# A gate of one element on GpSimd's queue, ahead of three of six early loads

## The chip, the cores and the metric

The kernel runs on one core of a Trainium2 chip. The metric is the device time of one execution in microseconds, the median over several runs. An execution's own time is a little longer than the span of its profile, which runs from the first to the last recorded instruction.

## The reference

The input is a sequence of 2048 rows with 512 features. Four residual layers follow one another: a convolution (A), a local attention (B), and both once more with the same weights. Each layer reads the layer norm of its input.

```python
def _A_ref(u, A_re, A_im, B_re, B_im, C_re, C_im, log_dt, Dskip):
    ...
    P = jnp.exp(logdA[:, :, None] * l[None, None, :])
    K = jnp.einsum("dn,dnl,dn->dl", Cc, P, dB).real      # one kernel of 2048 taps per feature
    ...
    Yf = Uf * Kf[None, :, :, :]                          # causal convolution by FFT of length 4096
    ...
def _B_ref(x, wqkv, wo):
    ...                                                  # 32 heads of 16; each row sees W=8 rows,
    logits = jnp.einsum("bhsd,bhswd->bhsw", q, kg) * scale   # 2 apart, itself and back
    attn = _softmax(logits, axis=-1)
    o = jnp.einsum("bhsw,bhswd->bhsd", attn, vg)
    return (lambda x, *d: x.transpose(*d))(o, 0, 2, 1, 3).reshape(B, S, D) @ wo

x = A_u
x = x + _A_ref(_layernorm(x, axis=-1), ...)
x = x + _B_ref(_layernorm(x, axis=-1), B_wqkv, B_wo)
x = x + _A_ref(_layernorm(x, axis=-1), ...)
x = x + _B_ref(_layernorm(x, axis=-1), B_wqkv, B_wo)
```

## The kernel before

The state `X` stays in SBUF as bf16, shaped 128 partitions × 16 slots × 512 features: row 16·p + j of the sequence is partition p of slot j. "The row sum of slot j" is the residual sum that the attention layer writes back into slot j of `X`.

The program has four stages, one per layer. `kernel_and_first_conv` builds the convolution kernels, transforms them and writes their spectra to DRAM, into `kt_scratch`: sixteen tiles, numbered (dc, c), with dc the feature block (0 to 3) and c a quarter of it. `b_layer` is the first attention, `a_layer` the second convolution, and `b_layer` again the second attention. `a_layer` doesn't build the spectra anew; it loads the sixteen tiles from `kt_scratch` into the tile `Kt`, for which there are eight buffers, and multiplies each with the transformed input (line 1172: `pa<-xc,Kt` on VectorE).

Each stage is written as a plan. `pl.op` notes an operation with its engine ("P" TensorE, "V" VectorE, "A" ScalarE, "G" GpSimd, "S" the DMA queue of SyncE, SP), an estimate of its time and what it depends on; `pl.either` notes several ways of doing one thing. `ORDERS` then holds, for each of the four plans, a list of operation numbers, written out ahead of time: it picks the way and fixes the order on every engine. The numbers count the operations as they are noted, ways not taken included. Semaphore waits follow from the data. As each engine works its queue in order across stages, instructions of the next stage can stand among those of the stage before, if the list of their stage and their place in the program's queue let them: GpSimd, with little to do, issues loads of `a_layer` while `b_layer` still runs.

A load of one tile (dc, c) is `load`, line 1222: two DMAs of 64 partitions each, 256 KB apiece, that put the tile's two planes into the upper and into the lower half of the partitions. For dc below 2 it is issued on GpSimd; the others go on SP, either in the same way (line 1222 as well) or as two smaller DMAs (line 1229) with two VectorE copies (line 1234) that fill in the other halves. Six loads are issued early on GpSimd, in the order (0,0), (0,3), (1,2), (1,1), (1,0), (1,3): twelve DMAs one behind another, once `kt_scratch` and the buffers are there. Two more early loads go on SP, after the last transposes of the attention. These eight fill the buffers; the other two loads of GpSimd, (0,1) and (0,2), wait until VectorE's products have freed theirs. The products run in the order (1,0), (1,3), (1,2), (1,1), (0,0), (0,3), and then the rest.

The end of `b_layer` is where the early loads run. VectorE multiplies values with weights (`prod`, line 1696), with four buffers for `prod`; TensorE sums the products in PSUM (`po`, lines 1711, 1720 and 1725). ScalarE writes `po` as bf16 into `ot` (line 1738), and a DMA on SP that transposes puts `ot` into `oT` (line 1743):

```python
nc.sync.dma_start(oT[:, fp, j * 256:(j + np) * 256].rearrange("f (b p) -> f b p", p=128),
                  box.pop(("ot", fp, j))[:, 0:np * 256], transpose=True)
```

Some parts of `oT` are written by TensorE and ScalarE instead (lines 1740 and 1753). TensorE multiplies `oT` with the output weights (`ps_o`, line 1808), and slot by slot the sum goes back to `X`. In the first attention, slots 8 to 15 are summed on VectorE in one of two ways, line 1783 straight from PSUM or line 1790 from a copy `sp` that ScalarE made (line 1787), or on TensorE, from where ScalarE copies it (line 1920). Slot 13 is the first of the two sums of line 1783. After it VectorE and ScalarE work out the norm of the rows (lines 200 to 229, 1930), which writes `U`, the input of `a_layer`. There, line 1118 begins the transform, the tile `Z` is transposed into `zt` on SP (line 1133) or by TensorE (line 1139), and the products follow.

`pst` holds statistics of the rows (lines 1360 and 1364), which the attention layers work out at their start; its part for slot 15 is not in use in the stretch that matters here.

Of the kernel before, what the change touches and what calls it, by code (L numbers as in the profile page):

```python
# [15 lines left out]
BF = mybir.dt.bfloat16  # L16
# [3 lines left out]
S = 2048  # L20
# [5 lines left out]
NJ = 16  # L26
# [95 lines left out]
def _bf(a):  # L122
    return np.ascontiguousarray(np.asarray(a, dtype=np.float32).astype(NPBF))
# [53 lines left out]
def b_weights(nc, const, wo):  # L177
    bones = const.tile([128, 4, 32], BF, name="sb_bones")
    wo_t = const.tile([128, 4, 512], BF, name="wo_t")
    VX = const.tile([128, 2, NV + NJ, 256], BF, name="VX")  # L180
    return dict(bones=bones, wo=wo_t, osrc=[wo[ft * 128:(ft + 1) * 128, :].rearrange("(h d) o -> d h o", d=DH) for ft in range(4)]), VX
# [50 lines left out]
def load_params(nc, pp, prm):  # L232
# [12 lines left out]

ORDERS = [
# [66 lines left out]
class Plan:  # L315
# [25 lines left out]
    def run(self):  # L341

        order = [int(i) for i in ORDERS[Plan.turn].split()]
        Plan.turn += 1
# [750 lines left out]
def a_layer(nc, tc, C, X, kt_dram, U):  # L1095

    with ExitStack() as es:
        vpool = es.enter_context(tc.tile_pool(name="a_vt", bufs=2))
        kp = es.enter_context(tc.tile_pool(name="a_kt", bufs=8, reuse_waits="tile"))
# [2 lines left out]
        zk = es.enter_context(tc.tile_pool(name="a_zt", bufs=6))  # L1102
        wk = es.enter_context(tc.tile_pool(name="a_wk", bufs=3))
        psA = es.enter_context(tc.tile_pool(name="a_psA", bufs=4, space=PSUM))
        ident, C2, IC, F1, F1T = C["ident"], C["C2"], C["IC2"], C["F1"], C["F1T"]
        Kl = {}
        pl = Plan(psA=4, Z=3, zt=6, xc=4, kt=8, pa=3, VT=2)
        box, zdone, tdone, vdone, Xq = {}, {}, {}, {}, {}
# [107 lines left out]
        def load(dc, c):  # L1216

            def go(eng):
                k = box["kt", dc, c] = kp.tile([128, 2, 1024], BF, name="Kt", tag="Kt")
                rows = kt_dram[dc, c]  # L1220
                for h in range(2):
                    eng.dma_start(k[64 * h:64 * h + 64], bass.AP(rows.tensor, rows.offset, [[1024, 64], [64 * 1024, 2], [1, 1024]]))
            if dc < 2:
                Kl[dc, c] = pl.op("G", 1.5, lambda: go(nc.gpsimd), pl.outer(("qk",)), take=("kt", dc, c), lag=4.0)
            else:
                def once():
                    k = box["kt", dc, c] = kp.tile([128, 2, 1024], BF, name="Kt", tag="Kt")
                    for h in range(2):
                        nc.sync.dma_start(k[64 * h:64 * h + 64, h], kt_dram[dc, c, 64 * h:64 * h + 64])

                def other():
                    k = box["kt", dc, c]
                    for h in range(2):
                        nc.vector.tensor_copy(k[64 - 64 * h:128 - 64 * h, h], k[64 * h:64 * h + 64, h])
                Kl[dc, c] = pl.either(("load", dc, c), lambda: pl.op("S", 1.15, lambda: go(nc.sync), take=("kt", dc, c), lag=4.0),
                                      lambda: pl.op("V", 0.84, other, pl.op("S", 1.15, once, take=("kt", dc, c), lag=3.5)))

        for dc in range(4):
            prev = []
            for j0, nj in ((0, 4), (4, 4), (8, 4), (12, 2), (14, 2)) if dc < 2 else ((0, 4), (4, 4), (8, 4), (12, 4)):  # L1240
                prev = [s1(dc, j0, nj, [pl.outer(("u", j)) for j in range(j0, j0 + nj)], *prev)]
            for c in range(4):
                load(dc, c)
            for c in range(4):
                turn(dc, c)
            for c in range(4):
                inverse(dc, c, product(dc, c, s2(dc, c)))
            nj = 4 if dc == 3 else 8
            for k in range(NJ // nj):
                final(dc, k, nj)  # L1250
# [3 lines left out]
def b_layer(nc, tc, C, X, Wt, VX, XT, pst, eps, ln, center, evac, done, VSTAT_Q):  # L1254

    with ExitStack() as es:
        oTp = es.enter_context(tc.tile_pool(name="b_oT", bufs=1))
        qk = es.enter_context(tc.tile_pool(name="b_qk", bufs=1))
# [16 lines left out]
        box = {}  # L1275
        pl = Plan(psA=2, psL=1, psO=2, prod=4, LT=3, sp=NSP, sm1=1, sm2=1, sm_m=1, sm_s=1, rdb=1)
# [498 lines left out]
        def tokens(fp, j, t, r):  # L1775
            if (fp, j // 8) == (1, 1):
                o = j * 256 + t * 128 + r
            else:
                o = j // 8 * 2048 + r * 16 + j % 2 * 256 + t * 128 + j % 8 // 2 * 32
            return oT[:, fp, o:o + 32]  # L1780
# [14 lines left out]
        def out(qt):  # L1795
            es = []
            for j in range(qt * 4, qt * 4 + 4):
                pool, ring = (psL, "psL") if j == 14 else (psO, "psO") if j == 15 else (psA, "psA")
                key = (ring, "o", j)

                def mm(begin, fts, res, j=j, pool=pool, ring=ring):
                    if begin:
                        box["o", j] = pool.tile([128, 512], F32, name="ps_o", tag=ring)
                    ps = box["o", j][:]
                    for ft in ([-1] if begin and res else []) + list(fts):
                        for r in range(0, 128, 32):
                            lhsT, rhs = (ident[:, r:r + 32], X[:, :, j, :]) if ft < 0 else (tokens(ft // 2, j, ft % 2, r), wo_t[:, ft, :])
                            nc.tensor.matmul(ps[r:r + 32], lhsT, rhs, start=(ft == -1 or ft == 0 and not res), stop=(ft == 3), skip_group_check=True)  # L1808

                def way(res, slow=False, j=j, key=key, mm=mm):  # L1810
                    if qt == 3:
                        a = pl.op("P", 0.68 if res else 0.46, lambda: mm(True, range(2), res), Od[0, j], Od["last", 1, 8], Wl.get("wo", []), take=key)
                        a = pl.op("P", 0.46, lambda: mm(False, range(2, 4), res), a, Od[1, j])
                    else:
                        a = pl.op("P", 1.14 if res else 0.91, lambda: mm(True, range(4), res), Od[0, j], Od[1, j], Wl.get("wo", []), take=key)
                    if res is None:
                        a = pl.op("A", 0.48, lambda: taken(j, box.pop(("o", j))[:]), a, take=("sp", j), drop=key)
                        if slow:
                            return pl.op("G", 1.2, lambda: summed_taken(j), a, lag=3.5, drop=("sp", j))
                        return pl.op("V", 0.33, lambda: added_taken(j), a, drop=("sp", j))  # L1820
                    fn = evac if res else added
                    return pl.op("A" if res else "V", 0.48 if res else 0.61,
                                 lambda: fn(j, box.pop(("o", j))[:]), a, drop=key)
                ways = [lambda: way(True), lambda: way(False)]
                es.append(pl.either(("out", j), *ways[::-1] if qt in ADD_Q else ways, lambda: way(None), lambda: way(None, True)) if qt in VSTAT_Q else way(True))
            done(pl, qt, es)

        if center:
# [45 lines left out]
def kernel(  # L1874
# [16 lines left out]
    nc = tc.nc  # L1891
    const = ctx.enter_context(tc.tile_pool(name="const", bufs=1))
    kt_dram = nc.dram_tensor("kt_scratch", (4, 4, 128, 1024), BF).ap()
    prm = dict(A_re=A_A_re, A_im=A_A_im, B_re=A_B_re, B_im=A_B_im, C_re=A_C_re, C_im=A_C_im, log_dt=A_log_dt,
               Dskip=A_Dskip)
    C = {}
# [5 lines left out]
    pst = const.tile([128, NJ, 2, 6], F32, name="pst")  # L1902
    X = kernel_and_first_conv(nc, tc, C, prm, A_u[0], const, kt_dram, eps, Wt)
    const2 = ctx.enter_context(tc.tile_pool(name="const2", bufs=1))
    ln = LnStats(nc, const2, [(0, D)], "a2", eps, "a2")
    ln.squares(const2)
    more, VX = b_weights(nc, const2, B_wo)
    for name, arr, dt in (("IC2", _bf(C["IC2"]), BF), ("minus", _bf(-np.eye(128)), BF), ("down", np.eye(128, k=1, dtype=np.float32), F32)):
        C[name] = load_const(nc, const2, name, arr, dt, nc.gpsimd)
    Wt.update(more)  # L1910
# [80 lines left out]
```

## Time and profile before

| | |
|---|---|
| median of 3 runs | 426.59 us (426.13 to 427.98) |
| profiled execution, own time | 428.47 us |
| profiled execution, span | 426.7 us |
| mean granted TensorE clock | 0.964 |
| busy: TensorE (PE), VectorE (DVE), ScalarE (ACT), GpSimd (POOL) | 83%, 92%, 77%, 7% |
| DMA queue of GpSimd's transfers (q0) | 3376 packets, 5.37 MB, 6.6% of 16 engines |
| DMA queue of SP's transfers (q1) | 97638 packets, 44.46 MB, 50.3% of 16 engines |

Times in a profile are counted from the span's start. A line such as L1696 is a line of the kernel before. A row of a timeline gives the start, the length, engine, line, operation, output and inputs, the count of instructions merged in it, and in brackets how long the engine sat idle before and who released it. SPq and POOLq are the queues from which SP and GpSimd issue DMAs. "To landing" is the time from the issue of a DMA until its completion is signalled.

### The profile page before, as it was taken

To read this page: it belongs to the slowest core of one execution; us is meant where nothing else is said; L and a number is where in the kernel's file an instruction comes from. 1 tells how busy PE (TensorE), PEld (TensorE's weight loads), DVE (VectorE), ACT (ScalarE), POOL (GpSimd) and SP (SyncE) were. 2 spreads that over 40 slices of the span, in tenths; PEclk is the share of its full clock that TensorE was granted. 3 is DMA by queue.
4 is the path that set the end of the run, shared out by engine and by line. 5 is a ranking of instruction groups with operands and counts; after the bars stand their busy time and mean duration, and the time that the engine had idled before them with its cause. 6 is when DMAs were issued, how large, how long until landed. Compare 5 with 4: busy or idle time off the path is not lost. (4 is left out here: it accounts for less than half of the span.)

```text
span 426.7 us, 13641 instructions
## 1 busy us (share of the span) xinstructions
PE 355.1 (83%) x5837; PEld 229.1 (54%) x5866; DVE 393.4 (92%) x652; ACT 326.5 (77%) x534; POOL 28.9 (7%) x98
## 2 busy tenths in 40 slices
PE   2259867987997889999985987899999999966994
PEld 1154655776786764446642533478774455642452
DVE  6999999999999788989999985999999999999994
ACT  7999999999998575579862794999976778762630
POOL 1000000000000200010000510020000010000321
PEclk9999989999999999999997996999999999995998
DMA  7996257697988775003335496099974000243496
GB/s 215 209 292 251 95 70 151 145 173 166 172 137 142 147 169 103 18 2 91 101 78 74 106 206 160 2 143 207 197 124 69 18 2 2 85 119 66 55 168 144
DMA packets 103538, 52.01 MB, mean 122 GB/s; under 512 B 82923, under 2 KB 95356, under 8 KB 103222
## 3 DMA queue, kind: packets, MB, share of 16 engines
q1 hardware_dynamic: 97638, 44.46, 50.3%
q0 software_dynamic: 3376, 5.37, 6.6%
q10 hardware_dynamic: 2464, 1.31, 1.1%
q8 instruction: 46, 0.75, 0.8%
q14 instruction: 14, 0.11, 0.1%
HBM read 19.30 MB, written 6.29 MB: 60 GB/s over the span
## 5 line engine op out<-in xcount | busy, mean ns | idle before, releaser
L1696 DVE TENSOR_TENSOR prod<-VX,L 128x512 bf16<-128x512 bf16 (+2 forms) x72 | 75.9, 1101 | 5.3 <-PE po L1725 4.8
L1520 DVE TENSOR_TENSOR prod<-qT,kT 128x4096 bf16<-128x4096 bf16 (+1 forms) x40 | 72.3, 1855 | 0.5 <-ACT kT L1426 0.3
L1808 PE MATMUL ps_o<-wo_t,oT 128*32 128x512 bf16 x512 | 34.2, 399 | 4.3 <-DMA oT<-ot 4.1
L1475 PE MATMUL ps_v<-wv,U 128*128 128x256 bf16 x256 | 31.6, 272 | 1.7 <-ACT VX L1486 1.0
L876 ACT CAST Z<-ps_s 128x1024 bf16<-128x1024 f32 (+1 forms) x36 | 32.0, 932 | 1.3 <-PE ps_s L873 1.1
L1421 PE MATMUL ps_qk<-U,wqk 128*128 128x512 bf16 x128 | 30.3, 380 | 0.7 <-ACT qT L1426 0.7
L1486 ACT ACTIVATE VX<-ps_v,rs 128x256 bf16<-128x256 f32 x64 | 26.8, 472 | 3.8 <-PE ps_v L1475 3.0
L1475 PEld LDWEIGHTS <-U 128*128 128x128 bf16 x256 | 24.5, 97 | 9.6 <-issue 5.1
L1440 PE MATMUL ps_qk<-U,wqk 128*128 128x512 bf16 x128 | 28.8, 379 | 0.8 <-ACT X L1210 0.8
L1531 PE MATMUL Lp<-prod,sb_bones 128*32 128x512 bf16 x256 | 22.8, 422 | 5.5 <-DVE prod L1520 5.5
L1738 ACT CAST ot<-po 128x1024 bf16<-128x1024 f32 (+1 forms) x15 | 14.4, 985 | 14.1 <-PE po L1711 10.5
L1808 PEld LDWEIGHTS <-oT 128*32 128x32 bf16 x512 | 13.3, 100 | 18.7 <-DMA oT<-ot 4.6
L1711 PE MATMUL po<-prod,sb_ident 32*32 32x512 bf16 x768 | 16.7, 419 | 8.0 <-DVE prod L1696 7.7
L1421 PEld LDWEIGHTS <-wqk 128*128 128x128 bf16 x128 | 11.8, 98 | 17.0 <-issue 4.8
L968 DVE TENSOR_TENSOR pa<-sp_u,sp_k 128x2048 bf16<-128x2048 bf16 x16 | 19.4, 1220 | 1.6 <-ACT sp_k L904 0.7
L1440 PEld LDWEIGHTS <-wqk 128*128 128x128 bf16 x128 | 12.4, 98 | 15.1 <-issue 1.1
L873 PE MATMUL ps_s<-KT,FK 128*128 128x128 bf16 (+1 forms) x360 | 18.8, 209 | 1.4 <-ACT KT L846 0.7
L1172 DVE TENSOR_TENSOR pa<-xc,Kt 128x2048 bf16<-128x2048 bf16 x16 | 18.9, 1219 | 0.6 <-PE vp L1184 0.3
L873 PEld LDWEIGHTS <-FK 128*128 128x128 bf16 x360 | 17.4, 98 | 3.0 <-issue 2.1
L893 PE MATMUL xp<-zt,sb_C 128*128 128x512 bf16 x45 | 15.2, 386 | 4.4 <-ACT zt L913 2.1
L982 PE MATMUL vp<-sb_IC,pa 128*128 128x128 bf16 x256 | 17.0, 219 | 2.2 <-DVE pa L968 1.2
L904 ACT CAST sp_k<-xp 128x1024 bf16<-128x1024 f32 x16 | 16.5, 1046 | 1.6 <-PE xp L893 0.7
(233 smaller groups left out, 864.4 us busy)
## 6 DMA issues: line engine op xcount, KB each, us to landing
kt_scratch<-sp_k SPq DMA_DIRECT2D x16, 256.0 KB, 3.1
Kt<-kt_scratch POOLq DMA_DIRECT2D x16, 256.0 KB, 7.1
sp_u<-sp_u SPq DMA_DIRECT2D x18, 128.0 KB, 2.8
X<-in_A_u_dram SPq DMA_DIRECT2D x8, 256.0 KB, 5.6
X<-in_A_u_dram SPq DMA_DIRECT2D x4, 512.0 KB, 5.2
Kt<-kt_scratch SPq DMA_DIRECT2D x8, 256.0 KB, 5.2
VX<-VX SPq DMA_DIRECT2D x4, 448.0 KB, 3.7
VX<-VX SPq DMA_DIRECT2D x4, 336.0 KB, 3.3
```

Of the source, the lines that this page charges most:

```text
L873: nc.tensor.matmul(ps[:, r, 0:n // 4, jj * 4:(jj + 1) * 4], w, x, start=(k == 0), stop=(k == len(todo) - 1))
L876: nc.scalar.copy(box["Z", kind, dc, b0][:, 0:n // 4, :, jq * 16:(jq + 1) * 16].rearrange("p g r k -> p r g k"), box.pop(("s1", kind, dc, j ...
L968: nc.vector.tensor_tensor(pr[:], box["U"][:, s:t + 1:t - s], k[:].unsqueeze(1).to_broadcast([128, 2, 1024]), ALU.mult)
L1172: nc.vector.tensor_tensor(pr[:], x[:].unsqueeze(1).to_broadcast([128, 2, 1024]), box.pop(("kt", dc, c))[:], ALU.mult)
L1421: nc.tensor.matmul(ps[:], wqk[:, ct, f0:f0 + 128], XT[:, ct // 2, 4 * s:4 * s + 4, ct % 2, :], start=(ct == 0), stop=(ct == 3))
L1440: nc.tensor.matmul(box[name][:, k * 512:k * 512 + 512], wqk[:, ct, f0:f0 + 128], XT[:, ct // 2, 4 * s:4 * s + 4, ct % 2, :], start=(ct == ...
L1475: nc.tensor.matmul(ps[:, jj].rearrange("p t h d -> p (t h d)"), XT[:, ct // 2, j + jj, ct % 2, :], wv[:, ct, fp * 256:(fp + 1) * 256], sta ...
L1486: nc.scalar.activation(out, ps, ACT.Identity, scale=r)
L1520: nc.vector.tensor_tensor(pr[:], windows(q, 0, 2), windows(kT[fp][:, a:a + n2, col(w):col(w) + 1024], -DIL * 128, 2), ALU.mult)
L1531: nc.tensor.matmul(Lp[r0:r0 + 32, w // 4, :], bones[:, w % 4 + k, :], pr[:, k, f2 - a, hb * 512:(hb + 1) * 512], start=(n == 1 and k == 0) ...
L1696: nc.vector.tensor_tensor(p2[:].rearrange("p w j t d h -> p w (j t) d h"), windows(v, -DIL * 256, taps), l.to_broadcast([128, taps, nj * 2 ...
L1808: nc.tensor.matmul(ps[r:r + 32], lhsT, rhs, start=(ft == -1 or ft == 0 and not res), stop=(ft == 3), skip_group_check=True)
```

## The change

A copy of one element on GpSimd reads partition 0, slot 13 of `X` and writes it into the unused part of `pst`. In the written-out order of the third plan it stands behind the third of the six early loads. It therefore waits for the sum in slot 13, and the last three early loads, (1,1), (1,0) and (1,3), stand behind it. As the copy reads slot 13, the later write of that slot (ScalarE, line 1210) waits for it in turn. The ways of a load are noted in another form, which shifts the numbers in the third list; the order on the other four engines stays as it was.

```diff
+GATES = (13,)
 ORDERS = [
...
-    "362 113 32 38 4 145 114 120 121 127 143 129 132 137 133 6 246 138 141 11 12 147 18 20 23 24 153 158 151 152 332 28 "
...
+    "388 127 32 47 4 165 52 128 134 135 141 160 143 146 151 147 6 272 152 155 11 12 170 18 20 23 24 179 184 177 178 358 "
...
+        held = C["held"]
...
+            key = ("kt", dc, c)
+            ways = [lambda: pl.op("S", 1.15, lambda: go(nc.sync), take=key, lag=4.0),
+                    lambda: pl.op("V", 0.84, other, pl.op("S", 1.15, once, take=key, lag=3.5))]
             if dc < 2:
-                Kl[dc, c] = pl.op("G", 1.5, lambda: go(nc.gpsimd), pl.outer(("qk",)), take=("kt", dc, c), lag=4.0)
...
+                ways.insert(0, lambda: pl.op("G", 1.5, lambda: go(nc.gpsimd), pl.outer(("qk",)), take=key, lag=4.0))
+            Kl[dc, c] = pl.either(("load", dc, c), *ways)
+
+        def gate(k, j):
+            pl.op("G", 0.1, lambda: nc.gpsimd.tensor_copy(held[0:1, k:k + 1], X[0:1, 0, j, 0:1]), pl.outer(("r", j)))
...
+            if dc == 0:
+                for k, j in enumerate(GATES):
+                    gate(k, j)
...
+                pl.mark(("r", j), es[-1])
...
+    C["held"] = pst[:, NJ - 1, 1, :]
```

More of the change, by code (lines that the diff above doesn't have):

```diff
@@ L1222, in go, with once, other @@
                     eng.dma_start(k[64 * h:64 * h + 64], bass.AP(rows.tensor, rows.offset, [[1024, 64], [64 * 1024, 2], [1, 1024]]))
-            if dc < 2:
-                Kl[dc, c] = pl.op("G", 1.5, lambda: go(nc.gpsimd), pl.outer(("qk",)), take=("kt", dc, c), lag=4.0)
[L1225 to L1236, printed above, removed]
+            def once():
+                k = box["kt", dc, c] = kp.tile([128, 2, 1024], BF, name="Kt", tag="Kt")
+                for h in range(2):
+                    nc.sync.dma_start(k[64 * h:64 * h + 64, h], kt_dram[dc, c, 64 * h:64 * h + 64])
+            def other():
+                k = box["kt", dc, c]
+                for h in range(2):
+                    nc.vector.tensor_copy(k[64 - 64 * h:128 - 64 * h, h], k[64 * h:64 * h + 64, h])
+            key = ("kt", dc, c)
+            ways = [lambda: pl.op("S", 1.15, lambda: go(nc.sync), take=key, lag=4.0),
+                    lambda: pl.op("V", 0.84, other, pl.op("S", 1.15, once, take=key, lag=3.5))]
+            if dc < 2:
+                ways.insert(0, lambda: pl.op("G", 1.5, lambda: go(nc.gpsimd), pl.outer(("qk",)), take=key, lag=4.0))
+            Kl[dc, c] = pl.either(("load", dc, c), *ways)
+        def gate(k, j):
+            pl.op("G", 0.1, lambda: nc.gpsimd.tensor_copy(held[0:1, k:k + 1], X[0:1, 0, j, 0:1]), pl.outer(("r", j)))
         for dc in range(4):
```

10 rows, old and new, of the table ORDERS are left out of this document.

## The prediction

> **What bounds the kernel now.** I read the page first, then the waits around the place of the change, the timelines of each engine there, the DMA view in short stretches, and last the same stage of the second attention layer.
>
> ```profile
> span 426.7 us, 13641 instructions
> PE 355.1 (83%) x5837; PEld 229.1 (54%) x5866; DVE 393.4 (92%) x652; ACT 326.5 (77%) x534; POOL 28.9 (7%) x98
> ```
> ```profile
> PE 18%; issue 3%; DVE 2%; ACT 1%; DVEq 0%; ACTq 0%
> ```
>
> VectorE (DVE) is busy for 92% of the span, so a microsecond is won where DVE sits idle. The chain of waits explains only 24% of the span (18 + 3 + 2 + 1), the part behind this stage, so I go by the waits of the stretch in which the first attention layer ends, 254 to 264 us:
>
> ```profile
> DVE prod L1696 <- PE po L1725: 4.8, 1, 4.8
> ...
> PE ps_o L1808 <- DMA oT<-ot: 4.1, 1, 4.1
> ```
>
> Two engines stand still here, and the release goes from a DMA (a transposing transfer of `ot` into `oT`) to TensorE (PE), and from PE to DVE. The timelines (a bracket holds the idle time before and its releaser), DVE first, then PE, ScalarE (ACT), the DMA issues of SP, and those of GpSimd (POOL):
>
> ```profile
> 251.04 3.98 DVE L1696 TENSOR_TENSOR prod<-VX,L 128x1024 bf16<-128x1024 bf16 x10
> 259.80 1.71 DVE L1696 TENSOR_TENSOR prod<-VX,L 128x512 bf16<-128x512 bf16 x4 [4.79 <-PE po L1725]
> ...
> 262.18 0.15 DVE L222 TENSOR_TENSOR ln_nb_a<-ln_nm,ln_rstd_a 128x4 f32<-128x4 f32 x1
> 263.25 0.69 DVE L1783 TENSOR_TENSOR X<-ps_o,X 128x512 bf16<-128x512 f32 x1 [0.92 <-PE ps_o L1808]
> ```
> ```profile
> 252.81 1.31 PE L1725 MATMUL po<-sb_ident,prod 128*128 128x128 bf16 x16
> 258.19 1.04 PE L1808 MATMUL ps_o<-wo_t,oT 128*32 128x512 bf16 x8 [4.05 <-DMA oT<-ot]
> ...
> 264.52 1.91 PE L1808 MATMUL ps_o<-wo_t,oT 128*32 128x512 bf16 x32
> ```
> ```profile
> 253.51 0.99 ACT L1738 CAST ot<-po 128x1024 bf16<-128x1024 f32 x1
> ```
> ```profile
> 255.73 0.19 ACT L1926 ACTIVATION_READ_ACCUMULATOR U<-X,ln_nm 128x1 f32 x1
> ```
> ```profile
> 248.87 8.64 SPq L1743 DMA_TRANSPOSE oT<-ot  x3
> 250.36 7.14 SPq L1743 DMA_TRANSPOSE oT<-ot  x2
> ```
> ```profile
> 239.36 5.37 POOL L1222 DMA_DIRECT2D Kt<-kt_scratch  x9
> ...
> 284.42 1.19 POOL L1222 DMA_DIRECT2D Kt<-kt_scratch  x2 [35.59 <-DVE pa L1172]
> ```
>
> POOL issues the twelve transfers of the six early loads from 239.36 on, the first nine without a pause (5.37 / 9 = 0.60 each). Three transposes follow on SP: T1 from 248.87, T2 from 250.36, T3 once ACT has written its `ot` (253.51 + 0.99 = 254.50) and T2 has been issued. How long they took to land, in the stretch 249.5:255 of the tile `oT` and then in the whole second layer, where no early load runs:
>
> ```profile
> DMA to landing us min/median/max: 7.8/8.0/8.3
> ```
> ```profile
> DMA to landing us min/median/max: 3.1/3.4/4.9
> ```
>
> The first row has T1 (8.3) and T2 (7.8): T2 landed at 250.36 + 7.8 = 258.16, and PE went on at 258.19. The queues say why, in 249:254 and then in 254.5:258:
>
> ```profile
> q0 software_dynamic: 342, 1.13, 102.6%
> ```
> ```profile
> q1 hardware_dynamic: 2385, 0.59, 118.7%
> q0 software_dynamic: 22, 0.06, 5.7%
> ```
>
> Between 249 and 254 us only POOL's queue q0 moved data; q1, which carries the transposes, has no row at all. It moved when q0 was nearly empty. That is the stall: two transposes standing behind a backlog of loads that nobody needs before 282.91 (below).
>
> **The change part by part.**
>
> *Three loads less ahead of the transposes.* A load is two transfers of 256 KB:
>
> ```profile
> Kt<-kt_scratch POOLq DMA_DIRECT2D x16, 256.0 KB, 7.1
> ```
> ```profile
> 239.40:247.50 8.10, 7.85 (x220) 4.14 (x211) 7.96 (x10) 6.38 (x18) 6.36 (x11) 1.00 0.87 198
> ```
> ```profile
> 248.90:254.00 5.10, 5.01 (x35) 2.45 (x32) 4.99 (x13) 5.04 (x14) 0.00 (x0) 1.00 1.03 227
> 254.00:258.20 4.20, 0.14 (x7) 0.02 (x5) 1.02 (x4) 1.92 (x5) 0.00 (x0) 0.75 1.20 183
> 258.20:263.20 5.00, 5.00 (x45) 2.56 (x49) 2.52 (x8) 1.69 (x4) 0.00 (x0) 0.53 0.93 227
> 263.20:277.20 14.00, 12.00 (x176) 6.41 (x170) 13.87 (x38) 12.96 (x26) 0.00 (x0) 1.00 0.02 6
> ```
>
> (Columns: stretch, length, busy time of PE, PEld, DVE, ACT, POOL, granted clock, DMA share, GB/s.) By 247.5 the queue had moved 8.10 × 198 = 1604 KB; the six transfers that stay early are 6 × 262 = 1573 KB. So q0 is empty some 1.4 us before T1 is issued. At the landing times of the second layer, T2 lands at 250.36 + 3.4 = 253.8. PE finishes its sixteen L1725 at 252.81 + 1.31 = 254.12: the 4.05 us wait is gone with 0.3 us to spare.
>
> *What is late next.* PE then does eight `ps_o`, then sixteen L1725 that empty the `prod` buffers DVE waits for. Their pace at full clock stands in the second layer (start to start 0.55 and 0.99 us):
>
> ```profile
> 410.83 0.61 PE L1808 MATMUL ps_o<-wo_t,oT 128*32 128x512 bf16 x8
> 411.38 1.07 PE L1725 MATMUL po<-sb_ident,prod 128*128 128x128 bf16 x16
> 412.37 1.91 PE L1808 MATMUL ps_o<-wo_t,oT 128*32 128x512 bf16 x32
> ```
>
> So L1725 starts at 254.70 and its first four matmuls end at about 254.95, just when DVE finishes its products (251.04 + 3.98 = 255.02). L1725 ends at 255.7; ACT is busy till 255.73 + 0.19 = 255.92, copies `oT` until about 256.5, and PE's next sixteen `ps_o` (0.06 us each, from 32 in 1.91) are done by about 257.1. DVE's own work between its two idle times is 262.18 + 0.15 − 259.80 = 2.53 us, which brings it to 257.6. DVE is the bound again, and its add into slot 13 moves from 263.25 to about 257.6. The DVE idle time that can go is 4.79 + 0.92 = 5.71 us, the ceiling of the gain. I leave 0.3 for hand-offs (an estimate: a third of the second idle time stays) and take **5.4 us**.
>
> Part of that is the clock. It was 0.75 in 254.00:258.20 and 0.53 in 258.20:263.20, after the idle time; I assume PE, with no hole, stays at 1.00.
>
> T3 would be issued at 254.53 and land at 254.53 + 3.4 = 257.9. Its readers are the 32 `ps_o` that began 264.52 − 263.25 = 1.27 us after the add, so at 258.9: covered. From there DVE is busy for 13.87 of 14.00 us, so nothing shrinks further and the 5.4 us are carried on whole; no later stage depends on absolute time.
>
> *The wait, and what stands behind it.* The copy waits for DVE's add into slot 13, which is the L1783 at 263.25 (first of two in this stage). Behind it on POOL stand the six transfers of three loads; the next POOL work is at 284.42 and waits for DVE's products. No other engine's order changes. ACT's write of slots 8 to 15 at the end of the stage must now also await the one-element read, which is tens of microseconds older. The trace has no copy on POOL; its nearest row is a transfer's issue, 0.60, and I take that. POOL having nothing else to do here, it could take several times as long unseen (the cover is counted next), and it removes nothing, so it can't be a gain.
>
> *Do the deferred loads come in time?* The add ends at 257.6 + 0.69 = 258.3, the copy at 258.9, six issues of 0.60 at 262.5. With the two loads that SP issues after T3 (four transfers) they are 10 × 262 = 2.62 MB; at 227 GB/s from about 257 they end at 268.6. Who needs the DMA engines or the data next:
>
> ```profile
> 277.21 11.14 SPq L1133 DMA_TRANSPOSE zt<-Z  x6
> ```
> ```profile
> 282.91 1.22 DVE L1172 TENSOR_TENSOR pa<-xc,Kt 128x2048 bf16<-128x2048 bf16 x1
> ```
>
> Moved up by 5.4 these are 271.8 and 277.5. The first two products read two of the three deferred tiles, so the cover is 3.2 us to the transposes and 9 us to the data: cost nothing.
>
> **Sum.** The profiled execution took 428.47 with a span of 426.7; less 5.4 that is 423.1 and 421.3. It lies 1.9 us (0.4%) above the median of the runs, 426.59, from which 5.4 gives **421.2**.
>
> **Rivals.** *The stall goes only in part.* If PE's clock still falls to half (it was granted 0.53 in the stretch), only the 4.05 us of waiting go: 422.5. If T2 also needs the slowest landing of the second layer, 4.9, it comes at 255.26, 1.1 us after PE: 423.6. For it: PE is less dense here than before. Against: the hole that preceded the slow clock is gone.
>
> *The transposes were not waiting for the loads.* Then the wait stays, and the time is 426.6. Against: q1 without a packet while q0 had 342. For: 249:254 shows only that they coincide. The Trainium skill, "DMA: Bandwidth & Descriptors", section "Queues, rings and completion order", has each DMA engine alternate between its queues packet by packet, so a transpose should have had its turn beside the loads, and its delay another cause; the trace does not agree, as no q1 packet moved in 5 us. That the copy reads something already complete, so that the gate opens at once, would give the same 426.6; but the add at 263.25 is the writer it waits for.
>
> *Slower: the deferred loads come too late.* POOL would have to be held up while DVE is dense (13.87 of 14.00 us), so that it begins its issues only when that stretch ends, at 271.8. The first is out at 272.4, and 1.57 MB at 227 GB/s keep q0 busy for 6.9 us, until 279.3; the `zt` transposes of 271.8 stand behind them as T1 did, and land at 279.3 + 3.4 = 282.7 and not at 271.8 + 3.4 = 275.2: 7.5 late. Less the 5.4 won, that is 2.1 lost, 428.7. It begins to cost when q0 is busy past 271.8, a microsecond for each, and turns the sign 5.4 us later. Against: in 239.40:247.50 DVE was busy for 7.96 of 8.10 us, and POOL's issues took their 0.60 each. The Trainium skill, "SBUF — State Buffer", section "SBUF: two separate sides", warns of just this: VectorE in its two-port modes locks GpSimd out, which then can't write its DMA descriptors. In this trace issues and data kept flowing beside a busy DVE.
>
> **How the numbers follow.** My forecast 0.70, with its own range from 420.3 (idle 5.71 gone, the rest run-to-run) to 422.4; the partial case 0.18; no effect 0.07; slower 0.05. The range, 420.0 to 424.0, takes in both faster cases, with 0.5 us for the spread of the runs, and leaves out the last two. About 0.5%, 2.1 us, is what a measurement of this kernel can tell from no change: faster is below 424.5, which holds the first case and nearly all of the second, 0.87; the same 0.08; slower 0.05.
>
> **What would show it.** Right: T1 to T3 land in 3 to 4 us, no PE wait on `oT` of more than 0.5 us, DVE's 4.79 and 0.92 gone, clock 1.00 through 263, the gate at about 258, q0 quiet from 247.5 until then and again before 271. Wrong: a transpose that still takes 8 us; a new wait of `ps_o` on T3; a product that waits for `Kt`; `zt` landing late.

## The result and the profile after

| | before | after |
|---|---|---|
| median | 426.36 us (425.68 to 427.98, 4 runs) | 421.89 us (421.17 to 422.17, 4 runs) |
| ratio, 95% interval | 1 | 0.9887 (0.9856 to 0.9919) |
| profiled execution, own time | 428.47 us | 421.17 us |

The change saves 4.5 us by the medians, 3.5 to 6.1 by the interval of the ratio. The predicted time was 421.2. Lines behind the change have new numbers: 1743 (the transposes) is now 1753, 1808 (`ps_o`) 1818, 1725 1735, 1783 (the add into slot 13) 1793, 1222 (the loads) 1224, 1133 and 1172 in the next layer 1135 and 1174; 1243 is the copy.

The ratios below leave out runs that are over 1.5% slower than the fastest of the same kernel; only experiment 5 has such runs.

The two profiled executions differ by 7.3 us, which is more than the change. The one of before was slower than all four of its timed runs, the one after is the fastest of its own. GpSimd issued its first early load already 1.74 us earlier (237.62 and not 239.36), ahead of everything that was changed, and SP its first transpose by as much (247.13 and not 248.87). So all comparisons of the stage below are made with 1.74 taken off.

The top of the page after, with the span and the busy times:

```profile
span 419.4 us, 13672 instructions
PE 355.7 (85%) x5866; PEld 226.9 (54%) x5866; DVE 393.0 (94%) x652; ACT 326.4 (78%) x534; POOL 29.1 (7%) x99
```

VectorE does as much work as before in a shorter span: 94% and not 92%. What vanished is idle time. The timelines at the end of the first attention, VectorE first, then TensorE:

```profile
249.38 5.43 DVE L1706 TENSOR_TENSOR prod<-VX,L 128x1024 bf16<-128x1024 bf16 x14
...
255.53 0.68 DVE L1793 TENSOR_TENSOR X<-ps_o,X 128x512 bf16<-128x512 f32 x1
```
```profile
252.39 0.61 PE L1818 MATMUL ps_o<-wo_t,oT 128*32 128x512 bf16 x8
252.94 1.07 PE L1735 MATMUL po<-sb_ident,prod 128*128 128x128 bf16 x16
...
257.63 1.48 PE L1818 MATMUL ps_o<-wo_t,oT 128*32 128x512 bf16 x24 [0.36 <-DMA oT<-ot]
```

None of the two VectorE rows has a bracket now: fourteen products run through, where after ten of them the engine had stood for 4.79 us, and the add into slot 13 does not wait. The eight `ps_o` at 252.39, which had waited 4.05 us, follow the matmuls ahead of them without a gap. A bracket of 0.36 us is left, at the third transpose.

The stages by windows (length, busy time of PE, PEld, DVE, ACT, POOL, granted clock, share of the DMA engines, GB/s), and what the DMA queues moved from 247 to 252 us:

```profile
245.80:247.20 1.40, 1.40 (x40) 0.47 (x22) 1.40 (x3) 1.16 (x3) 0.00 (x0) 1.00 0.04 12
...
252.30:256.40 4.10, 4.10 (x56) 1.87 (x53) 4.07 (x14) 4.05 (x11) 0.12 (x1) 1.00 0.63 76
256.40:261.40 5.00, 4.64 (x65) 1.64 (x67) 4.64 (x14) 4.45 (x9) 3.69 (x7) 1.00 1.00 204
```
```profile
q1 hardware_dynamic: 2112, 0.52, 55.2%
```

The DMA engines are all but idle in the 1.4 us ahead of the transposes (12 GB/s), and where q0 had 342 packets and q1 none, q1 alone has rows. The clock stays at 1.00. SP's transposes, GpSimd's queue, and the landing times of the three transposes:

```profile
247.13 6.89 SPq L1753 DMA_TRANSPOSE oT<-ot  x3
```
```profile
256.28 0.31 POOL L1243 CAST pst<-X 1x1 f32<-1x1 bf16 x1 [15.07 <-DVE X L1793]
256.54 3.59 POOL L1224 DMA_DIRECT2D Kt<-kt_scratch  x6
```
```profile
DMA to landing us min/median/max: 3.1/3.2/4.8
```

The first two land in 3.1 and 3.2 us (8.3 and 7.8 before); the third takes 4.8. The copy waits for the add into slot 13, as it should, and the six deferred transfers go out behind it.

### The profile page after: what moved, and what is told of

It is laid out like the page before. It is cut to its first block, busy times and chain, and to the rows that moved or that the text cites. A ratio compares the mean times of both kernels' runs of the same rounds, so it can differ in the third digit from the quotient of the medians.

```text
span 419.4 us, 13672 instructions
## 1 busy us (share of the span) xinstructions
PE 355.7 (85%) x5866; PEld 226.9 (54%) x5866; DVE 393.0 (94%) x652; ACT 326.4 (78%) x534; POOL 29.1 (7%) x99
## 5 line engine op out<-in xcount | busy, mean ns | idle before, releaser
L894 PE MATMUL xp<-zt,sb_C 128*128 128x512 bf16 x64 | 18.9, 379 | 4.2 <-ACT zt L914 2.3
```

## The experiments

**Theory.** The early loads delay the transposes, as their data stands ahead of theirs in the 16 DMA engines; the change wins by putting half of it behind. **Rivals.** The loads only coincide with the delay. The copy itself, or the new way of writing the loads, does it. The slow clock after the idle time is the loss. Only transposes suffer, or only queue q0 goes ahead. The loads cost the same later.

**1. The gate behind all six loads.** Everything of the change is there but the deferral: the copy's number in the third order moves behind the sixth load.

```diff
-    "388 127 32 47 4 165 52 128 134 135 141 160 ... 152 155 11 12 170 18 20 ... "
+    "388 127 32 47 4 165 128 134 135 141 160 ... 152 155 11 12 170 52 18 20 ... "
```

> The gate stands behind all six early loads instead of behind three; everything else is the changed kernel. My theory (the transposes T1 and T2 wait until GpSimd's queue q0 has no early load left): all twelve transfers are early again, so T1 and T2 land about 8 us after issue, PE waits about 4 us on oT, and the time is that of the kernel before, 426.4. The rival, that the gate itself or the renumbered plan brings the gain: 421.9.

Measured: 425.94 us (423.13 to 427.23, 10 runs), ratio 0.9970 (0.9941 to 0.9998). PE's row at slot 13's transpose, and VectorE's behind it:

```profile
256.46 1.05 PE L1818 MATMUL ps_o<-wo_t,oT 128*32 128x512 bf16 x8 [2.78 <-DMA oT<-ot]
```
```profile
258.09 1.71 DVE L1706 TENSOR_TENSOR prod<-VX,L 128x512 bf16<-128x512 bf16 x4 [3.51 <-PE po L1735]
```

The stall is back, and with it most of the time: VectorE idles for 3.51 us there. The copy and the other form of the loads bring 0.3% (0.6% at the end of the interval), not 1.1%. The wait is shorter than the 4 us expected, and the transposes land in 6.5 and 7.0 us, not 8. The loads moved faster in this execution: GpSimd issued the last of the twelve 7.98 us after the first (238.91 to 246.89), in the profile of before 8.87 us (239.36 to 248.23). So the size of the stall differs from one execution to the next.

**2. Five, and four loads early.** The same line, with the copy behind the fifth or the fourth load (`... 155 52 11 ...` and `... 160 52 143 ...`).

> Five loads early, one behind the gate. From the changed kernel's trace: first data at 238.8, 1.165 us a transfer, so ten transfers end at 250.5, after T1 (247.1) and T2 (248.6) are issued. In the kernel before T2 landed 3.8 us after q0 ran empty (254.4 to 258.16). So T2 lands at 254.3, PE wants it at 252.4: a stall of 1.9 us, 423.8, up to 424.5 if the clock falls too. Rival (the delay is a fixed one that any backlog brings): 426.

> Four loads early, two behind the gate. Eight transfers end at 248.2, between the issue of T1 and of T2; T2 would land at 252.0, just before PE wants it at 252.4. My theory: the time of the changed kernel, 421.9 (421.3 to 422.8). Rival (every load taken away brings its share, so the gain is in proportion): 421.9 + 4.5/3 = 423.4.

Measured: five early 422.28 us (421.60 to 423.96, 4 runs; ratio 0.9879, 0.9846 to 0.9912), four early 421.62 us (420.38 to 422.71, 4 runs; ratio 0.9868, 0.9832 to 0.9903). PE's rows of the two:

```profile
255.42 0.61 PE L1818 MATMUL ps_o<-wo_t,oT 128*32 128x512 bf16 x8 [1.14 <-DMA oT<-ot]
```
```profile
254.88 0.61 PE L1818 MATMUL ps_o<-wo_t,oT 128*32 128x512 bf16 x8 [0.50 <-DMA oT<-ot]
```

With six, five, four and three loads ahead of it PE waits 4.05 (2.78 in the first experiment), 1.14, 0.50 and 0 us for this transpose. The wait grows with the backlog, but not in proportion: putting off the sixth load alone was worth the most. For five early loads 1.9 us of wait and 423.8 us were expected, both too much; for four no wait was expected, but the time is as forecast. Times with three, four and five can't be told from one another.

**3. Three loads done twice.** The changed kernel, which transfers its three early loads a second time into the same buffers: as much early data as before, with the copy in its place.

```diff
+                if (dc, c) == (1, 2):
+                    for key2 in ((0, 0), (0, 3), (1, 2)):
+                        k, rows = box["kt", *key2], kt_dram[key2]
+                        for h in range(2):
+                            eng.dma_start(k[64 * h:64 * h + 64], bass.AP(rows.tensor, rows.offset, [[1024, 64], [64 * 1024, 2], [1, 1024]]))
```

> The changed kernel, but the three loads that stay early are each done twice (the same data into the same tile), so that twelve transfers stand on GpSimd's queue ahead of the transposes and the last three tiles still come after the gate. My theory: what counts is the amount on q0, not which tiles; the stall of about 4 us comes back, 426 (425.5 to 427). The rival, that it matters when the last three tiles are loaded or what GpSimd does later: 421.9.

Measured: 429.67 us (427.99 to 431.98, 10 runs), ratio 1.0064 (1.0038 to 1.0091).

```profile
257.19 1.04 PE L1823 MATMUL ps_o<-wo_t,oT 128*32 128x512 bf16 x8 [4.11 <-DMA oT<-ot]
```

The wait is that of before, 4.11 for 4.05 us, so it is the early data and not which buffers are filled. The time is longer than before by some 3 us. They are lost behind the stage, at 278 to 282 us, where VectorE is busy for 1.52 of 4.00 us: it waits for TensorE there, and TensorE for ScalarE's `Z`, though the order of the instructions on the three engines is that of the changed kernel. Whether the doubled loads bring this about isn't shown.

**4. Opened too early, or too late.** The gate reads slot 0's or slot 14's sum.

```diff
-GATES = (13,)
+GATES = (0,)      # and, in the other run, (14,)
```

> The gate reads slot 0's sum instead of slot 13's, so it opens early: the last three early loads are issued from about 248 us, beside the three DMA transposes of slots 12 to 14 (issued 247 to 253). The transposes are still ahead of them or level with them. Theory A (a transpose on SyncE's queue moves nothing while GpSimd's queue holds any transfer, whichever was issued first): the second and third transposes land after GpSimd's queue is empty at about 255, slot 13's sum is late again, PE waits 3 to 4 us and the time is about 426. Theory B (what was issued first goes first, whatever the queue): the first two transposes land in 3 to 4 us as in the changed kernel, only the third is late, by 2 to 3 us, and the time is 423 to 424.5. Theory C (the size of GpSimd's early traffic does not matter for the transposes at all): 421.9.

> The gate reads slot 14's sum, about 8 us after slot 13's, so the last three early loads are issued at about 265 and their data moves until about 273.5. The transposes of slots 12 to 14 are as in the changed kernel. Theory A (transposes are held while GpSimd's queue moves data): the transposes of Z on SyncE's queue, issued at 269.9, are held to about 273.5, some 3 us late; if they have slack it costs nothing, else up to 2 us: 422 to 424. The rival that loads held back too long make the first products wait: the data is needed from about 277, so a wait of PE of up to 2 us only if the loads are issued later than 268. If neither shows: 421.9.

Measured: slot 0 428.90 us (425.82 to 430.88, 9 runs), ratio 1.0047 (1.0017 to 1.0078); slot 14 424.77 us (422.05 to 427.94, 10 runs), ratio 0.9959 (0.9924 to 0.9994). First slot 0: GpSimd's queue, the landing of the three transposes, and PE:

```profile
249.09 3.55 POOL L1224 DMA_DIRECT2D Kt<-kt_scratch  x6
```
```profile
DMA to landing us min/median/max: 3.1/10.0/10.8
```
```profile
259.55 1.04 PE L1818 MATMUL ps_o<-wo_t,oT 128*32 128x512 bf16 x8 [6.18 <-DMA oT<-ot]
```

None of the three theories got this right. The first transpose, issued at 248.05, a microsecond ahead of the loads, landed in 3.1 us, which a strict "GpSimd's queue first" forbids. The second and third, issued among the loads and behind them, took 10.0 and 10.8 us, more than either theory had, and PE's wait is longer than before the change. So three loads in the wrong place hurt more than six.

With slot 14 the transposes of slots 12 to 14 are quick, but those of `Z` in the next layer, issued from 270.0 on, aren't (landing times of the stretch 269 to 282, and two of the waits from 246 to 300; in the changed kernel the landing times are 3.2/4.2/6.6):

```profile
DMA to landing us min/median/max: 5.0/9.2/11.7
```
```profile
PE xp L1161 <- DMA zt<-Z: 4.9, 2, 3.5
...
DVE pa L1174 <- DMA Kt<-kt_scratch: 1.4, 1, 1.4
```

The gate opened at 265.35 and not 256.28, and that cost 2.9 us of the median, a little more than the 0 to 2 expected.

**5. All six loads behind the gate.** The copy's number ahead of the first load (`... 127 52 32 47 ...`).

> The gate stands ahead of all six early loads: twelve transfers from about 255.5 behind slot 13's sum, together with SyncE's four. Nothing is left on GpSimd's queue before that, so the transposes of slots 12 and 13 land in 3.1 to 3.2 us as with three early loads: the gain of the stage is the whole one again. Twice the data of the changed kernel's deferred loads then stands behind the gate: done at about 273 to 274 instead of 269, so the transposes of Z start late by 3 to 4 us. Theory A: 422 to 424, the loss coming at the transposes of Z and not at slot 13. If deferring is free: 421.9.

Measured: 429.86 us (423.24 to 430.44, 10 runs), eight of them between 428.98 and 430.44, as is the profiled one, ratio 1.0007 (0.9956 to 1.0059). The queues from 270 to 275 us, and waits from 268 to 290:

```profile
q0 software_dynamic: 343, 1.10, 105.5%
```
```profile
PE xp L1161 <- DMA zt<-Z: 6.2, 2, 4.7
DVE VT L1189 <- PE vp L1186: 5.4, 1, 5.4
```

This is the picture of before, one layer on: q0 with 343 packets, q1 with none while the transposes of `Z`, issued from 269.67 on, stand there. The place of the loss was as expected, its size was not: against the changed kernel about 5 us by the ratios, 8 by the medians, and not 0 to 2. I had the data done by 274; GpSimd, with eight transfers out, had to wait for earlier ones before each of the last four, and its last was issued at 268.11.

**6. Only the clock.** The kernel before, with 18 idle products that keep TensorE busy while it waits.

```diff
+                        if center and begin and j == 13:
+                            for _ in range(18):
+                                nc.tensor.matmul(ps, ident[:], wo_t[:, 0, :], start=True, stop=True, skip_group_check=True)
```

> The kernel before, with 18 further products of 128 x 512 in PE's own wait ahead of slot 13's output projection, into the tile that the projection then starts anew: PE stays busy while it waits, the loads and transposes are as they were. Theory A (the stall is the late transpose; the half clock after it adds some): the wait of the projection on the transpose stays, slot 13's sum is as late as before, but the granted clock is full in 254 to 263 us; the time falls by up to 1.6 us, to about 425. Rival (the half clock is the loss, the wait alone is not): most of the 4.5 us come back, about 422.

Measured: 424.93 us (424.23 to 425.90, 10 runs), ratio 0.9979 (0.9951 to 1.0008). One window (the clock of before was 0.53 there) and VectorE's two places:

```profile
258.20:263.20 5.00, 5.00 (x70) 2.28 (x73) 4.06 (x13) 3.35 (x7) 0.00 (x0) 1.00 0.91 207
```
```profile
259.14 1.43 DVE L1696 TENSOR_TENSOR prod<-VX,L 128x512 bf16<-128x512 bf16 x4 [3.91 <-PE po L1725]
...
261.29 0.69 DVE L1783 TENSOR_TENSOR X<-ps_o,X 128x512 bf16<-128x512 f32 x1
```
```profile
258.15 0.61 PE L1811 MATMUL ps_o<-wo_t,oT 128*32 128x512 bf16 x8
```

The clock is full, and VectorE still idles for 3.91 us of its 5.71. The eight `ps_o` begin as late as before (258.15, before 258.19), but from there slot 13's add comes 3.14 us later and not 5.06. So the slow clock was about a third of the stall (1.8 to 1.9 us); the late transpose the rest. The time agrees less clearly: 1.9 us by the medians, 0.9 by the ratio, whose interval just reaches 1. The transposes were not quite as they were: the second landed in 6.7 us and not in 7.8, at about 257.2. The idle products end only at about 258.2, so up to a microsecond of the 3.91 may be theirs.

**7. A plain copy in the transposes' place.** The kernel before, with a store of 256 KB on SP just ahead of the first transpose.

```diff
+                if center and (fp, j) == (0, 12):
+                    nc.sync.dma_start(nc.dram_tensor("probe", (128, 1024), BF).ap(), box["ot", fp, j][:])
```

> The kernel before, with a plain store of 256 KB from the tile ot on SyncE's queue just ahead of the transpose of slot 12 (its output goes to a scratch tensor that nothing reads). It is issued at about 249 us, while GpSimd's queue still holds some five transfers. Theory 1 (only DMA transposes are held back by a backlog on GpSimd's queue; plain copies on two queues share the engines): SyncE's queue moves packets between 250 and 254, the store lands in 3 to 6 us, and only the transposes behind it land late, in 7 to 9 us. Theory 2 (whatever comes second waits for GpSimd's backlog): no packet of SyncE's queue between 250 and 254, and the store, too, lands only after 254. Time as before or up to 2 us more.

Measured: 426.31 us (1 run). The queues from 248 to 252 us, and the store, issued at 247.87 (column: KB, us to landing):

```profile
q0 software_dynamic: 287, 0.94, 99.9%
...
probe<-ot SPq DMA_DIRECT2D x1, 256.0 KB, 7.1
```

Again q1 has no row. The plain store waited like the transposes and landed after 7.1 us: Theory 1, that only transposes are held back, fell. Theory 2 was off by two microseconds: q1 has packets from 252 us on, as q0 runs out.

**8. A backlog on a third queue.** The changed kernel, with 2.5 MB of stores from a constant on ScalarE's queue, ahead of slot 6's sum and, in another run, of slot 7's.

```diff
+        side = nc.dram_tensor("side", (3, 128, 4096), BF).ap()
...
+            if j == 6:          # and, in the other run, 7
+                wide = C["F1T"][:].rearrange("p a b c -> p (a b c)")
+                for k, n in enumerate((4096, 4096, 2048)):
+                    nc.scalar.dma_start(side[k, :, 0:n], wide[:, 0:n])
```

> The changed kernel, with 2.5 MB of plain stores from a constant in SBUF to a scratch tensor on ScalarE's queue, issued after slot 6's sum, so that the transposes of slots 12 and 13 (issued at 247.1 and 248.4) fall into their data, some 11 us. Theory 1 (a transpose is held back by any backlog of plain copies, whichever queue it is on): the transposes land late, after the stores, in 7 us or more, and the stall at slot 13 is back (2 to 5 us). Theory 2 (it is GpSimd's software queue that goes first): they land in 3 to 6 us, PE waits under 1.5 us.

> The changed kernel, with the same 2.5 MB of plain stores on ScalarE's queue, but issued after slot 7's sum, at 240 to 242 us, when GpSimd's first six transfers (237.6 to 241.2) are all but issued. Theory 1 (the engines serve the queues about in the order of issue, whichever queue it is): GpSimd's 1.5 MB first, to about 246, then ScalarE's stores, to about 252; the transposes of slots 12 and 13 (247.1 and 248.4) come behind them and land in 6 us or more; PE waits 2 to 4 us for slot 13's transpose, DVE behind it, and the time is 424.5 to 426, though GpSimd's early loads are three as in the changed kernel. Theory 2 (only GpSimd's software queue goes ahead of SyncE's): the transposes land in 3 to 5 us beside the stores, PE waits under 1 us, 422.

Measured: 421.89 us (1 run) and 424.58 us (422.55 to 426.65, 10 runs; ratio 0.9956, 0.9928 to 0.9983). Both missed their mark. In the first the stores were issued at 234.2 to 235.1 and over by 242. In the second their issue held ScalarE up (3.59 us of idle time), the whole stage came later, and the first transpose, at 250.09 and not 247.13, met only their end. That 424.58 lies in the range of Theory 1 is chance: the three transposes landed in 3.1 to 4.9 us, and the time was lost ahead of them. But the queues met GpSimd's loads (from 239.5 to 242 in the first run, where the loads were issued from 238.06 on, after all the stores; from 242 to 246 in the second, where both were issued in turn, 237.37 to 240.96 and 239.50 to 243.7):

```profile
q10 hardware_dynamic: 172, 0.75, 101.3%
```
```profile
q10 hardware_dynamic: 138, 1.01, 64.1%
q0 software_dynamic: 177, 0.59, 36.4%
```

In the first q0 is the one that has no row: GpSimd's queue had no right of way here, it waited for ScalarE's. In the second both move.

**9. SP's two early loads on GpSimd too.** The third transpose took 4.8 us, and SP's loads ran beside it. Here they stand behind the gate: their numbers in the third order, 388 and 272, move behind the sixth load of GpSimd.

```diff
-    "388 127 32 47 4 165 52 128 ... 147 6 272 152 155 11 12 170 18 20 ... "
+    "127 32 47 4 165 52 128 ... 147 6 152 155 11 12 170 388 272 18 20 ... "
...
+                if (dc, c) in ((3, 2), (2, 0)):
+                    eng = nc.gpsimd
```

> The changed kernel, with SyncE's two early loads of Kt (four transfers, issued from 254.1 right behind the third transpose) also on GpSimd's queue behind the gate. In the changed kernel the third transpose took 4.8 us beside them and PE waited 0.36 us. Theory (the third transpose is slowed by whatever plain copies run beside it): it lands in 3.1 to 3.5 us, PE's wait is gone, slot 13's sum comes up to 0.3 us earlier. GpSimd's deferred transfers are ten instead of six and end at 269 to 270 as before, for the data is the same; the time is 421.5 to 422, which can hardly be told from the changed kernel's. Rival (the backlog on GpSimd's queue holds the transposes of Z, issued at 269.9, more than SyncE's part of it did): they land in over 6 us and the time is 423 to 425.

Measured: 422.41 us (421.57 to 422.88, 6 runs), ratio 0.9909 (0.9885 to 0.9934). The landing times of the three transposes:

```profile
DMA to landing us min/median/max: 3.1/3.2/4.6
```

The third still takes 4.6 us with nothing beside it, so SP's loads were not its reason, and nothing is gained. Why it takes longer than the first two is open. No version tried here was shown to beat the changed kernel.

## Why the prediction was right

*Three loads less leave q0 empty before the first transpose.* Right: 12 GB/s in the 1.4 us ahead of it, and landings of 3.1 and 3.2 us for the 3.4 taken from the second layer. That it is the loads that did it is shown by experiments 1 to 3: the copy alone leaves the stall, three loads done twice bring it back, and the wait falls with each load put off.

*PE's and VectorE's pace.* Right: eight `ps_o`, then L1735 0.55 us later, as in the second layer, at full clock. The add was to come at 257.6, which is 255.86 with the 1.74 us taken off; it came at 255.53. So all the idle time went, and the 0.3 us left for hand-offs weren't needed. In the stage 5.98 us were won (263.25 − 255.53 − 1.74), more than the 5.71 called a ceiling: the four products behind the wait had taken 1.71 us, and in the run of fourteen they take 5.43 − 3.98 = 1.45. In the medians 4.5 us were won. The predicted 5.4 lies within the 3.5 to 6.1 of the interval; the runs don't settle it more finely. But the 5.71 came from one execution, in which the loads moved slowly (experiment 1). With all six loads early VectorE idled for 3.51 us in experiment 1 and for 3.96 + 0.71 in experiment 7, so a typical stall is probably smaller, and the 5.4, taken off the median of the runs, probably somewhat too much.

*Part of it is the clock.* Right, and experiment 6 gives the size: 1.8 of 5.7 us. The rival in which the clock stays slow would have left about that much.

*T3 is covered.* Wrong by a little. It landed in 4.8 us and not in 3.4, and PE waited for it, 0.36 us. The row quoted for the second layer had a 4.9 at its upper end; I took the median for T3 and the upper end for a rival on T2 only. VectorE felt 0.22 us of it.

*The copy.* 0.31 us and not 0.60, with nothing behind it that cared. It waited for the add, as stated. The Trainium skill's warning that VectorE locks GpSimd out ("SBUF — State Buffer", section "SBUF: two separate sides") had no weight for the issues: six in 3.59 us, 0.60 each, in the window where VectorE was busy for 4.64 of 5.00 us. The page speaks of VectorE in its two-port modes, and the trace doesn't show which modes ran, so the warning itself isn't tested.

*The deferred loads come in time.* Right, with less to spare than stated. They were to end at 268.6, or 266.9 with 1.74 off. In the changed kernel GpSimd's queue was done at about 269, just ahead of the first transpose of `Z`, at 269.88 (this row is q0 from 269 to 271):

```profile
q0 software_dynamic: 5, 0.01, 2.6%
```

The 3.2 us of cover were about one. Ten transfers at 227 GB/s was the term that was mis-sized; over their whole time it was 190 (the columns are those of the windows above):

```profile
255.50:269.50 14.00, 11.80 (x170) 5.95 (x163) 13.59 (x40) 13.10 (x27) 3.81 (x7) 1.00 1.01 190
```

*The rival that ends slower* named the right mechanism, deferred loads that hold back the transposes of `Z`, and the wrong trigger. GpSimd was not held up. But experiment 5, with six loads behind the gate, lost 5 to 8 us against the changed kernel by just this, and experiment 4, with the gate 9 us later, 2.9. The price was about right: I had it cost a microsecond for each that q0 is busy past 271.8, or 270.1 with 1.74 off; with q0 busy to about 276 that makes 6.

*Transposes that don't wait for the loads.* This rival fell. The price that went with it for a gate that opens at once, 426.6, was wrong too: slot 0's gate in experiment 4 opened at 248.68 and cost more, 428.90. The packet-by-packet turn that the Trainium skill, "DMA: Bandwidth & Descriptors", section "Queues, rings and completion order", gives each DMA engine among the queues that it has work for isn't seen where the transposes waited. The traces show when a transfer was issued, not when its packets were ready at the engines, so they don't refute it. Three stretches of 4 to 5 us show one queue alone at work while the other had transfers issued: 342 packets to none before the change, 287 to none in experiment 7, 343 to none in experiment 5. Two show both at work, experiment 8's second and the changed kernel itself, from 258 to 264 us, where SP's loads (issued 254.12 to 257.64) met the deferred ones (256.54 to 260.13):

```profile
q1 hardware_dynamic: 380, 0.71, 61.4%
q0 software_dynamic: 159, 0.52, 43.0%
```

The prediction said that the transposes stand "behind a backlog of loads". That held. What it left unsaid, and the runs of gates and stores narrow down without settling it, is in which sense behind: all five stretches, and experiment 8's first, fit the order of issue, whichever queue it is. A queue whose transfers were all issued later had no packet; where two queues issued in turn, both moved. It was inferred from these, not tried by itself: the run meant for it, ScalarE's stores ahead of the transposes, missed. And it is not the whole: in experiment 4 transposes issued among six loads took 10 us, longer than the loads ahead of them explain.

## What to carry to other kernels

A transfer that nobody needs soon is not free because its queue is idle: the DMA engines behind the queues are shared (q0 alone kept all 16 busy between 249 and 254 us, 102.6%), and in most stretches seen here what was issued first went out first. Look in the windows ahead of each latency-bound transfer for a queue that is full, find out when its data is really needed, and hold it back by a small dependence on work that ends right after the critical transfers. The place of the gate is a window with two edges: 7.6 us too early it lost more than the whole gain, 9 us too late over half of it.

## What the runs showed of the hardware that was not expected

- A plain store of 256 KB behind a backlog on another queue took 7.1 us, the same as the transposes beside it (7.1 to 7.5): transposes aren't singled out.
- GpSimd's queue waits too: for 2.5 us (239.5 to 242, experiment 8) it moved nothing while ScalarE's stores had 172 packets.
- Transposes that ran among large plain copies were slowed more than those that waited until the copies were over: 10.0 and 10.8 us in experiment 4, 7.8 and 8.3 before the change.
- Idle products that keep TensorE busy during a wait kept the granted clock at 1.00 where it had been 0.53, and slot 13's add came 1.9 us sooner after the projection's start (3.14 and not 5.06 us), though the projection began no earlier.
